# Attention block: x transposed mostly by transfers, late weights loaded later, one of 24 planned orders built

## The chip, the cores and the metric

The kernel runs on one core of a Trainium2 chip. The time is device microseconds of one execution; the median of three executions before the change is 361.78 us (361.48 to 361.86). The engines are called PE (TensorE, matrix products), ACT (ScalarE), DVE (VectorE), POOL (GpSimd) and SP (SyncE, which only issues transfers here).

## The reference

x is 2048 x 448, 16 heads of 28 columns each, all in bf16. There is no mask.

```
qkv = (x @ wqkv)                  # 448 -> 3 x 448, split into q, k, v per head
scores = q @ k.T * 28 ** -0.5     # 16 heads, 2048 x 2048 each
p = softmax(scores)               # over the keys
o = p @ v
out = o (heads side by side) @ wo
```

## The kernel before

**Tiling.** Heads are taken in four groups of four; a head has 32 rows (28 and 4 of padding) of the 128 partitions. Queries are cut into four chunks of 512 (c), keys into 16 tiles of 128, x into four blocks of 512 rows (b). A set is one group and one query chunk: 16 sets, each with 4 heads x 16 key tiles = 64 halves of 128 keys by 512 queries. There are 1024 halves.

**Start.** x is loaded row by row (L140) and transposed by PE with an identity (L621), 16 transposes of 128 x 112 per block, since the 448 columns are cut into four parts of 112. ACT copies the first half of a block from PSUM to SBUF (L629), DVE the second (L627); the result is XT. Then come the projections. `mm_proj` (L298) makes K and Q of a group with 16 matmuls per block of 512 (four parts of the columns, four heads); for group 0 it reads WG, an early load of the few weight columns needed, and later WRAW, the full weights (L136). `v_job` (L305) makes V. `k_first` makes K of group 0 for one block, with its square (L324), the norm over a head (L409) and its maximum (L414). `q_job` and `qn_first` make the first Q and its norm; the bound from both norms is subtracted from the scores through spare rows of Q, so that no maximum over the scores is taken. QP holds Q with these rows. It is cleared by DVE (L194), gets constant rows by 16 small transfers on SP (L198, from a tile offs), the rows of Q by four (L661) and the bound's rows, su, by two (L502). Until all this has landed, the first set's scores are made in two matmuls, from z and from su, in place of one from QP.

**Main phase.** A scores step (`emit_s`, L730) makes two halves for ACT, and often one for DVE. ACT takes the exponential of two halves at a time (L928, 128 x 1024). DVE makes an approximate exponential of one half by integer arithmetic (L943), with two shifted copies of four halves (L1014, or for one of them a clear and an accumulating transfer by POOL, L979 and L990) that are averaged in the next product. `do_pv` (L1073) multiplies with V. When a set is complete, its sum is divided: a gather and a scatter on SP, a reciprocal on DVE, four broadcasts on SP (rr) and a product on POOL (L1123). When a query chunk has all groups, `oproj_job` multiplies by WO and stores the rows. Row p*16 + 4*b + t of x, and of the output, belongs to partition p and column t of block b.

**Order.** The order of the instructions is written by a planner within the kernel: it keeps a clock for each engine (`free`), a table of times at which events happen (`evt`), durations as constants, and picks for the engine that is earliest the next operation by priority. Loads enter as fixed times. The planner fixes the order in each engine's queue; on the chip each engine runs its queue in order and waits on semaphores. `dve_ok` decides whether DVE takes another half; `pick_dve` sends a shifted copy ahead when it is older than AGE (2.5 us).

```
for n, t in (("x", 0), 4.9), (("G", 1), 6.9), (("G", 0), 6.9), (("x", 1), 6.2), (("x", 2), 8.0), (("x", 3), 9.3), \
        (("W", 2), 10.9), (("W", 0), 12.0), (("W", 1), 13.2):
    evt[n] = (t, "DMA")
```

**Queues at the start.** SP issues half of each x block, one WG, the three WRAW, L198, L661 and L502 in this order; ACT issues the other halves and the other WG, then loads its table. POOL clears V (L209, L210), clears WO (L216) and loads it with 16 transfers (L219).

Of the kernel before, what the change touches and what calls it, by code (L numbers as in the profile page):

```python
# [16 lines left out]
LAT = 0.2  # L17
# [20 lines left out]

@with_exitstack
def kernel(  # L40
# [16 lines left out]
    CK = D // CC  # L57
# [11 lines left out]
    NXB = NKT // XB  # L69
    SHIFT = (0, 43, 85)  # L70
# [20 lines left out]
    NSET = G * NQC  # L91
    GH = 2
# [6 lines left out]
    out_perm = out2.rearrange("(p t) d -> p t d", t=NKT)  # L99
# [7 lines left out]
    XT = [[big.tile([CK, CC // 2, QW], BF16, name=f"XT{b}_{k}") for k in range(2)] for b in range(NXB)]  # L107
# [15 lines left out]
    xs = [big.tile([P, XB, D], BF16, name=f"xs{b}") for b in range(NXB)]  # L123
    QP = [[[big.tile([P, QW], BF16, name=f"QP{c}_{k}_{z}") for z in range(2)] for k in range(2)] for c in range(NQC)]
    OTL = [big.tile([P, QW], BF16, name=f"OTL{c}") for c in range(NQC)]

    def otile(g, c):
        if g < G - 1:
            return xs[c][:].rearrange("p t d -> p (t d)")[:, g * QW:(g + 1) * QW]
        return OTL[c][:]  # L130

    wq3 = wqkv.rearrange("(cc p) n -> p cc n", p=CK)
    x3 = x2.rearrange("(p t) c -> p t c", t=NKT)

    def load_w(t, eng):
        eng.dma_start(out=WRAW[t][:, :, 0:D], in_=wq3[:, :, t * D:(t + 1) * D])  # L136

    def load_x(b, eng, k=0, n=1):
        w = XB // n
        eng.dma_start(out=xs[b][:, k * w:(k + 1) * w, :], in_=x3[:, b * XB + k * w:b * XB + (k + 1) * w, :])  # L140

    def load_w0(t, eng):
        eng.dma_start(out=WG[t], in_=wq3[:, :, t * D:t * D + HG * Dh + WPAD])
# [33 lines left out]
    offs = wk.tile([P, 2 * QW], BF16, name="pt", bufs=NPT)[0:2, 0:QW]  # L177
# [12 lines left out]
    nc.vector.memset(offs, OFFS)  # L190
    for c in range(NQC):
        for k in range(2):
            for z in range(2):
                nc.vector.memset(QP[c][k][z][:], 0.0)  # L194
    for z in range(2):
        for c in range(NQC):
            for k in range(2):
                nc.sync.dma_start(out=QP[c][k][z][HP * k + Dh + NQC - 1 - c:P:2 * HP, :], in_=offs)  # L198
# [4 lines left out]
    for t in range(3):  # L203
        nc.gpsimd.memset(WRAW[t][:, :, D:D + WPAD], 0.0)

# [9 lines left out]
    for gg in range(G):  # L215
        nc.gpsimd.memset(WO[:, gg, :], 0.0)  # L216
    for h in range(H):
        g, i = divmod(h, HG)
        nc.gpsimd.dma_start(out=WO[HP * i:HP * i + Dh, g, :], in_=wo[h * Dh:(h + 1) * Dh, :])  # L219
# [7 lines left out]
    def pair_tile(tg):  # L227
        return psum.tile([P, 2 * QW], F32, name=tg, tag=tg, bufs=1)

    def bank_tile(tg):  # L230
        return psum.tile([P, QW], F32, name=tg, tag=tg, bufs=1)


    free = {"PE": 0.0, "ACT": 0.0, "DVE": 0.0, "SP": 0.0, "POOL": 26.0}
    port = {"DVE": 0.0, "POOL": 0.0}
    evt = {}
    res = {"a0": 0.0, "a1": 0.0, "d0": 0.0, "d1": 0.0, "o": 0.0, "m": 0.0}
    ops = {"PE": [], "ACT": [], "DVE": [], "SP": [], "POOL": []}
    cnt = {"step": 0, "half": 0}
    held = {}  # L240
    cur = {"c_end": 0.0, "s": 0, "u": 0, "o": None, "oset": 0, "pv": 0, "half": 0, "o_open": False}
    parts = {}

    def add(eng, dur, emit, **k):
        op = Op(eng, dur, emit, **k)
        ops[eng].append(op)
        return op

    def ready(op):
        if cnt["step"] < op.gate or (op.acq == "m" and op.gives[0][0] == "O" and left() < OLAST):  # L250
            return None
        if op.acq == "m" and op.pri > 5 and ("KN0", NQC - 1) not in evt:
            return None
        r = 0.0
        for n in op.need:
            if n not in evt:
                return None
            t, e = evt[n]
            r = max(r, t + (0.03 if e == op.eng else LATS.get((e, op.eng), LAT)))
        if op.acq is not None:  # L260
            if res[op.acq] is None:
                return None
            r = max(r, res[op.acq])
        return r + op.lag

    def run(op, t):
        op.emit()
        if op.eng == "PE":
            note(t, op.cols)
        end = t + op.dur  # L270
        if op.eng == "PE" and main_on():
            cur["c_end"] = end
        if op.port:
            port[op.eng] = end
        for n in op.gives:
            evt[n] = (end + op.land, op.eng)
        if op.after is not None:
            op.after(end)
        if op.acq is not None:
            res[op.acq] = None  # L280
        if isinstance(op.rel, tuple):
            parts.setdefault(op.rel[0], []).append(end + LATS.get((op.eng, "PE"), LAT))
            if len(parts[op.rel[0]]) == op.rel[1]:
                res[op.rel[0]] = max(parts.pop(op.rel[0]))
        elif op.rel is not None:
            res[op.rel] = end + LATS.get((op.eng, "PE"), LAT)
        ops[op.eng].remove(op)
        return end


    KAt, QAt, sqt, kst, kmt = {}, {}, {}, {}, {}

    def mm_proj(ps, t, g, c, ccs):
        for cc in ccs:
            for i in range(HG):
                h = g * HG + i
                w = WG[t] if g == 0 else WRAW[t]
                nc.tensor.matmul(out=ps[HP * i:HP * (i + 1), :], lhsT=w[:, cc, h * Dh:h * Dh + HP],  # L298
                                 rhs=XT[c][cc // 2][:, cc % 2, :], start=(cc == 0), stop=(cc == CC - 1),
                                 tile_position=(0, HP * i))  # L300

    def quarters(out, lhsT, rhs, start, stop, **k):
        for i in range(P // HP):
            r = slice(HP * i, HP * (i + 1))
            nc.tensor.matmul(out=out[r, :], lhsT=lhsT[:, r], rhs=rhs, start=start, stop=stop, tile_position=(0, HP * i), **k)  # L305

    def after_shared(m):

        if "shared" in cur:
            tc.add_manual_dep(m.ins, cur["shared"].ins.name,  # L310
                              mybir.DependencyInfo(mybir.DependencyClass.Sync, mybir.DependencyReason.DATA),
                              reason="GpSimd's pass stays behind VectorE's")

    def new_sq(key):
        sqt[key] = wk.tile([P, QW], BF16, name="sq", tag="sq", bufs=4)
        return sqt[key]

    def square(key, src):
        t = new_sq(key)
        after_shared(nc.gpsimd.tensor_tensor(out=t[:], in0=src, in1=src, op=ALU.mult))  # L320

    def act_square(key, mask):
        t = new_sq(key)
        nc.scalar.activation(out=t[:], in_=held[key][:, 0:QW], func=ACT.Square, scale=mask[:, 0:1])  # L324

    def k_job(g, sc, bank, pri, gate=0, split=2):
        key = ("K", g, sc)
        n = CC // split

        def mm(part):  # L330
            if part == 0:
                held[key] = bank_tile(bank) if bank[0] != "a" else pair_tile(bank)
            mm_proj(held[key][:, 0:QW], 1, g, sc, range(part * n, (part + 1) * n))

        def evac():
            KAt[(g, sc)] = big.tile([P, QW], BF16, name=f"KA{sc}", tag=f"KA{sc}", bufs=2)
            src = held[key][:, 0:QW]
            nc.vector.tensor_scalar(out=KAt[(g, sc)][:], in0=src, scalar1=kmask[:, 0:1],  # L338
                                    scalar2=ones[:, 0:1], op0=ALU.mult, op1=ALU.add)

        for p in range(split):
            add("PE", n * D_WAVE, lambda p=p: mm(p), pri=pri, gate=gate, cols=448 * n,
                need=[("XT", sc, 0), ("XT", sc, 1), ("W", 1)] + ([key + (p - 1,)] if p else []), gives=[key + (p,)],
                acq=bank if p == 0 else None)
        add("DVE", 0.72, evac, need=[key + (split - 1,)], gives=[key], rel=bank, pri=pri)
        add("POOL", 1.08, lambda: square(key, KAt[(g, sc)][:]), need=[key], gives=[("ksq", g, sc)], pri=pri, port=True)

    def kn_job(g, bank, pri, gate=0):
        key = ("KN", g)

        def mm(sc):
            if sc == 0:
                held[key] = bank_tile(bank) if bank[0] != "a" else pair_tile(bank)
            quarters(held[key][:, 0:QW], maskK[:, sc, :], sqt.pop(("K", g, sc))[:], sc == 0, sc == NQC - 1)
# [1026 lines left out]
```

## Time and profile before

| | |
|---|---|
| median of 3 executions | 361.78 us |
| profiled execution | 361.72 us |
| its span, first to last instruction | 359.9 us |
| granted clock of PE | 0.998 of full speed |
| exponentials on ACT (L928) | 358, 329.7 us, with pairs of halves |
| halves on DVE (L943) | 308 (278 from d, 30 from m) |
| first exponential / last ends | 19.39 us / 351.3 us |
| POOL's set-up ends | 23.0 us |

The span is shorter than the time by what lies around the first and the last instruction. Busy time is the sum of an engine's instructions within the span; a group of the profile joins the instructions of one line, engine and operation, with their count, their mean duration and the idle time ahead of them. The chain of waits goes back from the last instruction to what released each step. SPq and ACTq are transfers being issued from the queues of SP and ACT; such an issue occupies the queue, and the transfer lands later.

### The profile page before, as it was taken

Reading aid. Unit: us, or ns where it says so; the run is one execution under the profiler, and the core shown is the slowest. Engines: PE = TensorE matmul, PEld = TensorE weight load, DVE = VectorE, ACT = ScalarE, POOL = GpSimd, SP = SyncE. Lnnn points to the kernel's source line nnn. Section 1 sums busy time; section 2 is a strip of 40 time slices with the busy share of each in tenths; the row PEclk is TensorE's granted clock in tenths of the full one; section 3 lists DMA queues with packets and bytes.
Section 4 is the critical chain, followed back from the end, with each engine's and each line's share of the span. In section 5 each row is a group of like instructions: output and inputs, shape, how many; then the busy total and the mean of one; then the engine's idle time right before and its main releaser. Section 6 shows DMA issues by size and latency. Waiting matters only on the chain.

```text
span 359.9 us, 11256 instructions
## 1 busy us (share of the span) xinstructions
PE 343.1 (95%) x4520; PEld 111.3 (31%) x4521; DVE 335.4 (93%) x617; ACT 341.1 (95%) x373; POOL 170.2 (47%) x213
## 2 busy tenths in 40 slices
PE   8999999999999999999999999999889999999995
PEld 4533233332234322332232222222222222222233
DVE  8689999999989999999899999999999999999863
ACT  3789999999999999999999999999999999999991
POOL 8951353655444483545635765465546362521010
PEclk9999999999999999999999999999999999999999
DMA  8620063555636765365577646377857685672111
GB/s 242 142 47 15 21 125 86 113 107 105 135 75 129 148 124 113 89 132 108 117 143 149 120 91 137 78 152 158 177 116 156 128 176 129 142 147 66 34 51 54
DMA packets 24017, 41.17 MB, mean 114 GB/s; under 512 B 8604, under 2 KB 15004, under 8 KB 23964
## 3 DMA queue, kind: packets, MB, share of 16 engines
q0 software_dynamic: 8432, 29.24, 42.0%
q1 hardware_dynamic: 14348, 10.07, 10.3%
q10 hardware_dynamic: 1184, 1.14, 1.0%
q8 instruction: 35, 0.57, 0.6%
q14 instruction: 18, 0.15, 0.1%
HBM read 7.58 MB, written 1.96 MB: 27 GB/s over the span
## 4 chain that ended last, share of the span: by engine, by line
PE 37%; ACT 30%; DVE 23%; issue 9%; DMA 1%; DVEq 0%; ACTq 0%
ACT pt L928 30%; PE a L730 12%; DVE I L943 10%; PE o L1073 10%; PE m L305 5%; DVE J L1014 5%; PE m L298 4%; DVE V L579 2%; DVE V L566 2%; DVE KA L338 1%; PE o L643 1%; PE d L730 1%; DVE QA L460 1%; DVE o_sb L1100 1%; PE d L621 1%
## 5 line engine op out<-in xcount | busy, mean ns | idle before, releaser
L928 ACT ACTIVATE pt<-a 128x1024 bf16<-128x1024 f32 x358 | 329.7, 1129 | 2.9 <-PE a L730 1.3
L943 DVE TENSOR_SCALAR I<-d 128x512 int16<-128x512 f32 x278 | 181.0, 680 | 10.1 <-PE d L730 8.8
L730 PE MATMUL a<-QP,KA 32*128 32x512 bf16 (+1 forms) x704 | 137.3, 381 | 8.9 <-ACT pt L928 8.0
L1073 PE MATMUL o<-pt,V 128*32 128x512 bf16 x716 | 105.2, 384 | 0.0
L730 PE MATMUL d<-QP,KA 32*128 32x512 bf16 (+1 forms) x273 | 95.7, 383 | 0.8 <-DVE I L943 0.2
L730 PEld LDWEIGHTS <-KA 32*128 32x128 bf16 (+1 forms) x1041 | 46.1, 91 | 143.5 <-issue 141.7
L990 POOL DMA_DIRECT2D J<-I x55 | 49.6, 902 | 73.0 <-DVE I L943 49.6
L1073 PE MATMUL o<-J,V 128*32 128x512 bf16 x616 | 82.7, 384 | 0.0
L979 POOL MEMSET J<- 128x1024 int32 x55 | 60.1, 1094 | 36.7 <-PE d L730 12.0
L1014 DVE TENSOR_SCALAR J<-I 128x2048 int16<-128x2048 int16 x99 | 73.9, 764 | 0.6
L1073 PE MATMUL o<-I,V 128*32 128x512 bf16 x308 | 64.3, 384 | 0.1
L1073 PEld LDWEIGHTS <-V 128*32 128x32 bf16 x1640 | 30.8, 94 | 48.2 <-issue 45.1
L1123 POOL TENSOR_TENSOR xs<-o_sb,rr 128x512 bf16<-128x512 f32 x12 | 16.9, 1404 | 27.3 <-DVE J L1014 26.9
L298 PE MATMUL m<-XT,WRAW 112*32 112x512 bf16 x384 | 29.6, 384 | 0.2 <-DVE QA L460 0.2
L320 POOL TENSOR_TENSOR sq<-QA 128x512 bf16<-128x512 bf16 x15 | 16.8, 1122 | 23.1 <-DVE QA L460 17.8
L305 PE MATMUL m<-WRAW,XT 112*32 112x112 bf16 (+1 forms) x768 | 20.7, 230 | 0.3 <-DVE KA L338 0.3
L943 DVE TENSOR_SCALAR I<-m 128x512 int16<-128x512 f32 x30 | 20.3, 678 | 0.0
L320 POOL TENSOR_TENSOR sq<-KA 128x512 bf16<-128x512 bf16 x12 | 14.2, 1185 | 9.4 <-DVE J L1014 8.5
L305 PEld LDWEIGHTS <-XT 112*32 112x32 bf16 x768 | 12.3, 96 | 11.5 <-issue 11.4
L305 PE MATMUL m<-WO,xs 128*32 128x448 bf16 x156 | 12.5, 358 | 0.0
L730 PE MATMUL m<-QP,KA 32*128 32x512 bf16 (+1 forms) x30 | 11.5, 384 | 0.0
L460 DVE CAST QA<-m 128x512 bf16<-128x512 f32 x15 | 10.2, 683 | 0.7 <-PE m L298 0.7
(116 smaller groups left out, 207.3 us busy)
## 6 DMA issues: line engine op xcount, KB each, us to landing
J<-I POOLq DMA_DIRECT2D x55, 512.0 KB, 4.9
rr<-scr SPq DMA_DIRECT2D x60, 64.0 KB
QP<-QA SPq DMA_DIRECT2D x60, 28.0 KB
out_dram<-osb SPq DMA_DIRECT2D x12, 112.0 KB
WRAW<-in_wqkv_dram SPq DMA_DIRECT2D x3, 392.0 KB
xs<-in_x_dram ACTq DMA_DIRECT2D x4, 224.0 KB
xs<-in_x_dram SPq DMA_DIRECT2D x4, 224.0 KB
QP<-su SPq DMA_DIRECT2D x32, 2.0 KB
```

What stands on the lines that cost most here:

```text
L298: nc.tensor.matmul(out=ps[HP * i:HP * (i + 1), :], lhsT=w[:, cc, h * Dh:h * Dh + HP], rhs=XT[c][cc // 2][:, cc % 2, :], start=(cc == 0), s ...
L305: nc.tensor.matmul(out=out[r, :], lhsT=lhsT[:, r], rhs=rhs, start=start, stop=stop, tile_position=(0, HP * i), **k)
L320: after_shared(nc.gpsimd.tensor_tensor(out=t[:], in0=src, in1=src, op=ALU.mult))
L460: nc.vector.tensor_copy(out=t[:], in_=held[key][:, 0:QW])
L730: nc.tensor.matmul(out=out_ap, lhsT=KAt[(g, j // XB)][r, (j % XB) * P:(j % XB + 1) * P], rhs=q[r, :], start=(n == 0), stop=(n == len(terms ...
L928: nc.scalar.activation(out=pt[:], in_=ps[:], func=ACT.Exp, scale=LN2 / 128.0)
L943: nc.vector.tensor_scalar(out=dst, in0=pd[:], scalar1=BIAS, scalar2=0.0, op0=ALU.add, op1=ALU.max)
L979: m = nc.gpsimd.memset(ch[1][:].bitcast(I32), fill)
L990: after_shared(nc.gpsimd.dma_start(out=ch[1][:, w], in_=ch["I"][:, w], accum_op=ALU.add))
L1014: cur["shared"] = nc.vector.tensor_scalar(out=r[:, w], in0=ch["I"][:, w], scalar1=float(SHIFT[k]), scalar2=None, op0=ALU.add)
L1073: nc.tensor.matmul(out=o[HP * i:HP * (i + 1), :], lhsT=VT[e["k"]][g, j // XB][:, j % XB, HP * i:HP * (i + 1)], rhs=e["ap"], start=(SETMM[k ...
L1123: m = nc.gpsimd.tensor_tensor(out=otile(g, c), in0=st["o_sb"][:], in1=st["rr"][:], op=ALU.mult)
```

## The change

- x: block 0 is loaded and transposed by PE as before, in parts of 128 columns (0, 128, 256 and 320 on; the last part overlaps the third by 64 columns). Blocks 1 to 3 come transposed by transfers on SP: one for columns 320 to 447 of all three blocks (XE), and one per block for columns 0 to 383. The weights' last part has zeros in its first 64 rows, so each projection still has four parts.
- Rows: block b is now rows 512*b to 512*b + 511; for blocks 1 to 3 row t*128 + p belongs to partition p. The output is stored in the same way.
- Weights: each load is two transfers; both WG go to ACT's queue. W0 and W1 are issued on SP after QP is complete for the first set.
- QP: half of it is cleared by POOL, and 14 of the 16 small transfers go to POOL's queue. offs has its own tile.
- WO: its clears wait for the last Q of group 0; its 16 loads go to SP in the planned part and the output projection waits for them.
- Planner: other due times, other PSUM banks for the first norms, QPRI 3.05; the whole plan is a function, run 24 times without emitting anything, with a random term in `dve_ok` (up to 0.4 us) and in the age (up to 1 us) except for number 0, and then once for the number whose latest engine clock is earliest.

The diff, without the lines that only move to the right:

```
-    CK = D // CC
+    CK = P
+    CT = D - CK
+    NPL = 1
+    NSEED = 24
-    out_perm = out2.rearrange("(p t) d -> p t d", t=NKT)
+    def out_at(c, tq, n=1):
+        o = out2[c * QW:(c + 1) * QW]
+        o = o.rearrange("(p t) d -> p t d", t=XB) if c < NPL else o.rearrange("(t p) d -> p t d", p=P)
+        return o[:, tq:tq + n, :] if n > 1 else o[:, tq, :]
...
+    def load_w(t, eng, n=D):
+        dst = WG[t] if n < D else WRAW[t][:, :, 0:D]
+        cols = slice(t * D, t * D + n)
+        eng.dma_start(out=dst[:, 0:CC - 1, :], in_=wqkv[0:(CC - 1) * CK, cols].rearrange("(cc p) n -> p cc n", p=CK))
+        eng.dma_start(out=dst[CC * CK - D:CK, CC - 1, :], in_=wqkv[(CC - 1) * CK:D, cols])
+    def load_x(b):
+        rows = slice(b * QW, (b + 1) * QW)
+        nc.sync.dma_start_transpose(out=XT[b][:], in_=x2[rows, 0:(CC - 1) * CK])
-    load_x(0, nc.sync, 0, 2)
-    load_x(0, nc.scalar, 1, 2)
-    for b in range(1, NXB):
-        load_x(b, nc.sync, 0, 2)
-        load_x(b, nc.scalar, 1, 2)
-        if b == 1:
-            load_w0(1, nc.sync)
-            load_w0(0, nc.scalar)
+    for b in range(NPL):
+        for eng, k in ((nc.sync, 0), (nc.scalar, 1)):
...
+    for t in range(2):
+        nc.vector.memset(WG[t][0:CC * CK - D, CC - 1, :], 0.0)
+    for t in (1, 0):
+        load_w(t, nc.scalar, HG * Dh + WPAD)
+    nc.sync.dma_start_transpose(out=XE[:], in_=x2[NPL * QW:S, CT:D])
+    for b in range(NPL, NXB):
+        load_x(b)
     load_w(2, nc.sync)
-    load_w(0, nc.sync)
-    load_w(1, nc.sync)
...
-            for z in range(2):
-                nc.vector.memset(QP[c][k][z][:], 0.0)
-    for z in range(2):
-        for c in range(NQC):
-            for k in range(2):
-                nc.sync.dma_start(out=QP[c][k][z][HP * k + Dh + NQC - 1 - c:P:2 * HP, :], in_=offs)
+            nc.vector.memset(QP[c][k][0][:], 0.0)
+    nc.gpsimd.memset(offs[:], OFFS)
+    offs_rows(0, 0, nc.sync)
...
+        nc.gpsimd.memset(WRAW[t][0:CC * CK - D, CC - 1, 0:D], 0.0)
...
+    for c in range(NQC):
+        for k in range(2):
+            nc.gpsimd.memset(QP[c][k][1][:], 0.0)
+    for z in range(2):
+        for c in range(NQC):
+            if c + z:
+                offs_rows(c, z, nc.gpsimd)
...
-    free = {"PE": 0.0, "ACT": 0.0, "DVE": 0.0, "SP": 0.0, "POOL": 26.0}
+    free = {"PE": 0.0, "ACT": 0.0, "DVE": 0.0, "SP": 0.0, "POOL": 25.6}
...
+    for n, t in [(("x", 0), 4.9), (("x", 1), 99.0)] + [(("XT", k, h), 8.9 + 1.8 * (k - NPL)) for k in range(NPL, NXB) for h in range(2)] + \
+            [(("G", 1), 6.7), (("G", 0), 6.7), (("W", 2), 14.2)]:
         evt[n] = (t, "DMA")
...
+    for gg in range(G):
+        add("POOL", 0.5, lambda gg=gg: clear_wo(gg), need=[("QA", 0, CL)], gives=[("WZ", gg)], pri=95, port=True)
+    for h in range(H):
+        add("SP", 0.55, lambda h=h: load_wo(h), need=[("WZ", h // HG)], gives=[("WO", h)], pri=9, land=2.5)
-    k_first(0, "a0", None, "DVE", "ACT", 1.5)
-    k_first(1, "a1", "o", "ACT", "ACT", 3.05, late=("ksq", 0, NQC - 1))
-    k_first(2, "d0", "a0", "ACT", "ACT", 3.1, late=("ksq", 0, NQC - 1))
-    k_first(3, "d1", "o", "DVE", "ACT", 3.2, late=("QA", 0, 0))
+    k_first(0, "a0", "o", "DVE", "ACT", 1.5)
+    k_first(1, "a1", "a0", "ACT", "ACT", 3.05, late=("ksq", 0, NQC - 1))
+    k_first(2, "d0", "o", "ACT", "ACT", 3.1, late=("ksq", 0, NQC - 1))
+    k_first(3, "d1", "a0", "DVE", "ACT", 3.2, late=("QA", 0, 0))
...
+    for t in range(2):
+        add("SP", 1.2, lambda t=t: load_w(t, nc.sync), need=["QP00"], gives=[("W", t)], land=6.0, pri=3)
...
-    return fin <= free["ACT"] + D_EXP * (len(exps) + max(0, left() // 2 - 2)) + 0.2
+    return fin <= free["ACT"] + D_EXP * (len(exps) + max(0, left() // 2 - 2)) + 0.2 + shake(0.4)
...
-    if can_add and t > adds[0][0]["at"] + AGE:
+    if can_add and t > adds[0][0]["at"] + AGE + shake(1.0):
...
+    d = Dry()
+    ends = {k: plan(d, d, d, d, d, d, k, True) for k in range(NSEED)}
+    seed = min(ends, key=lambda k: ends[k])
+    plan(nc, tc, psum, big, wk, dram, seed, False)
```

More of the change, by code (lines that the diff above doesn't have):

```diff
@@ L1 @@
+import random
 from contextlib import ExitStack
@@ L266, in run @@
[L266 to L288, printed above, removed]
@@ L291 @@
[L291 to L305, printed above, removed]
@@ L307, in after_shared @@
[L307 to L346, printed above, removed]
@@ new lines, in turn, with do_s @@
+        def turn(t):
+            return max(t, cur["c_end"] + D_TURN)
+        def do_s(t):
+            s = act_set()
+            if s >= NSET:
+                return None
+            q = qa_ready(s)
+            if q is None or q > t:
+                return None
+            got = d_more(s, t, True) if left() >= 16 or chain["cur"] is not None else []
+            used = {g[2][1] for g in got}
+            step = []
+            for x in range(2):
+                own = [i for i in (2 * x, 2 * x + 1) if i not in used and remain[s][i]]
+                step.append(take(s, max(own, key=lambda i: (len(remain[s][i]), (i + cur["u"]) % 2))))
+            bank = s_bank()
+            ps = pair_tile(bank)
+            emit_s([(ps[:, k * QW:(k + 1) * QW], step[k]) for k in range(2)] + [(g[1][:], g[2]) for g in got], t)
+            outst[s] += 2
+            res[bank] = None
+            t = turn(t)
+            end = t + D_S
+            exps.append((end + LATS[("PE", "ACT")], ps, bank, step))
+            cur["u"] += 1
+            cnt["half"] += 2
+            return max(end, put_d(got))
@@ new lines, in close, with used_up, j1_free, add_ok @@
+        def close(ch, m):
+            ch["m"] = m
+            ch["at"] = free["DVE"]
+            adds.append([ch, m, 2 if ch["far"] else 1])
+            if ch["far"]:
+                accumulate(ch, m)
+        def used_up(ch, k):
+            return ch["m"] is not None and ch["got"][k] == ch["m"]
+        def j1_free():
+            return len(chain["all"]) < NJ or used_up(chain["all"][-NJ], 1)
+        def add_ok(a):
+            if a[2] == 1:
+                return True
+            n = chain["all"].index(a[0])
+            return n < NCH2 or used_up(chain["all"][n - NCH2], 2)
@@ new lines, in far_chain, with emit, accumulate, landed @@
+        def far_chain(ch):
+            n = len(chain["all"])
+            fill = SHIFT[1] * 65537
+            def emit():
+                m = nc.gpsimd.memset(ch[1][:].bitcast(I32), fill)
+                after_shared(m)
+            ch["id"] = n
+            add("POOL", 1.05, emit, gives=[("fill", n)], pri=20, port=True)
+        def accumulate(ch, m):
+            w = slice(0, m * QW)
+            ch["acc"] = None
+            def emit():
+                after_shared(nc.gpsimd.dma_start(out=ch[1][:, w], in_=ch["I"][:, w], accum_op=ALU.add))
+            def landed(end):
+                at = ch["acc"] = end + ACC_LAND
+                for n in range(m):
+                    pending.append({"step": ch["steps"][n], "k": 1, "ap": ch[1][:, n * QW:(n + 1) * QW].bitcast(BF16),
+                                    "ready": at, "pt": None, "ch": ch})
+            evt[("I4", ch["id"])] = (free["DVE"], "DVE")
+            add("POOL", 0.88, emit, need=[("fill", ch["id"]), ("I4", ch["id"])], gives=[("acc", ch["id"])], pri=10, port=True)
+            ops["POOL"][-1].after = landed
@@ new lines, in flush, with do_add @@
+        def flush():
+            ch = chain["cur"]
+            if ch is not None and ch["done"] == ch["n"] and not any(remain[ch["s"]]):
+                chain["cur"] = None
+                close(ch, ch["n"])
+        def do_add(t):
+            ch, m, k = adds[0]
+            w = slice(0, m * QW)
+            if k == 2:
+                ch[k] = wk.tile([P, HG * QW], I16, name="J2", bufs=NCH2)
+            r = ch[k]
+            cur["shared"] = nc.vector.tensor_scalar(out=r[:, w], in0=ch["I"][:, w], scalar1=float(SHIFT[k]), scalar2=None, op0=ALU.add)
+            end = port["DVE"] = t + m * QW * 0.00026 + 0.068
+            for n in range(m):
+                pending.append({"step": ch["steps"][n], "k": k, "ap": r[:, n * QW:(n + 1) * QW].bitcast(BF16),
+                                "ready": end + LATS[("DVE", "PE")], "pt": None, "ch": ch})
+            adds[0][2] += 1
+            if adds[0][2] == NTERM:
+                adds.pop(0)
+            return end
@@ new lines, in plan, with filler @@
+        if dry:
+            return max(free.values())
+        s = NSET - 1
+        g, c = set_gc(s)
+        o = cur["o"]
+        HW = QW // 2
+        banks = held["early"]
+        more = sorted((op for op in ops["PE"] if op.gives[0][0] == "E"), key=lambda op: op.gives[0][1:])
+        def filler(n, to=XB):
+            for op in [op for op in more if op.gives[0][1] < to][:n]:
+                op.emit()
+                more.remove(op)
+        osb_last = [VT[1][0, hf].rearrange("p t e -> p (t e)").bitcast(F32) for hf in range(2)]
```

1801 lines of the change are left out of this document (893 added, 908 removed).

## The prediction

> **What bounds the kernel now.** I read the page's busy shares and slices first, then ScalarE (ACT) by stretches, then the chain of waits over the first 20 us, then SyncE's (SP's) timeline. From the page, the busy shares and two rows of the slices (a digit is the busy share of 9 us, in tenths):
>
> ```profile
> PE 343.1 (95%) x4520; PEld 111.3 (31%) x4521; DVE 335.4 (93%) x617; ACT 341.1 (95%) x373; POOL 170.2 (47%) x213
> ...
> DVE  8689999999989999999899999999999999999863
> ACT  3789999999999999999999999999999999999991
> ```
>
> Three engines run at 93 to 95%, and ACT's only poor slices are the first three and the last. ACT alone, from its first exponential (19.39 us) on; the second figure after the stretch is busy time:
>
> ```profile
> 19.39:24.95 5.56, 4.90 (x6) 1.00 0.27 63
> 24.95:351.30 326.35, 324.78 (x353) 1.00 0.55 113
> 351.30:359.90 8.60, 0.97 (x2) 0.91 0.16 56
> ```
>
> From 24.95 to 351.30 us ACT idles 1.57 us in all. It runs 358 exponentials at 329.7 / 358 = 0.921 us each, back to back. So the end is the first exponential, plus some 332 us, plus a tail of 8.6 us. What can move is the first exponential, the 0.66 us lost in the ramp, and how many exponentials ACT is given. The chain of waits before the first one (start, duration, what):
>
> ```profile
> 9.00 1.03 PE d L621 x16
> 10.03 0.98 PE a L298 x16
> 11.01 0.58 PE o L621 x8
> 11.59 0.21 PE a L409
> 11.81 0.45 PE m L621 x8
> 12.25 0.98 PE d L298 x16
> 13.23 0.32 PE o L409
> 13.55 0.98 PE m L298 x16
> 14.53 0.32 PE a L409
> 14.85 1.01 PE d L298 x16
> ```
>
> L298 is a projection (K of blocks 1, 2, 3 and Q of block 0), L621 are TensorE's transposes of x, L409 the key norms. TensorE works without a pause until 15.86 us. From there to the first exponential lie 3.53 us (square, norm, maximum, root, scaling, first scores), which the change leaves as they are.
>
> **The change, part by part.**
>
> *Transposes taken away.* Blocks 1 to 3 lose 48 of 64 transposes, three copies on ACT (1.00 us, L629) and three on VectorE (DVE, 0.68 us, L627). Block 1's transposes lie before K0, which waits for DVE's copy of block 0 (7.20 + 0.66 = 7.86 us) anyway: worth nothing. Those of blocks 2 and 3 are the three L621 pieces above: 1.03 + 0.58 + 0.45 = 2.06 us. The copies lie beside TensorE's chain and count no more. TensorE would then end K3 at 15.86 - 2.06 = 13.80 us, and ACT would start at 17.33.
>
> *Transfers put in their place.* SP issues four transposing transfers: XE (128 columns of 1536 rows) and three blocks of 512 rows by 384 columns, 0.39 MB each, 1.57 MB together, beside and behind block 0 and the first weights (0.67 MB). The trace has no transposing transfer; the nearest rows are two of the transfers by microsecond (last figure GB/s) and one of the page's issues (KB each, us to landing):
>
> ```profile
> 4.00:5.00 1.00, 1.00 (x3) 0.29 (x2) 0.99 (x4) 0.01 (x1) 0.89 (x4) 1.00 1.06 382
> 13.00:14.00 1.00, 1.00 (x21) 0.40 (x17) 0.54 (x2) 0.69 (x1) 1.00 (x4) 1.00 0.57 126
> ...
> J<-I POOLq DMA_DIRECT2D x55, 512.0 KB, 4.9
> ```
>
> In the four microseconds before 4.00 us 30, 122 and 384 GB/s moved 0.54 MB, so the 0.67 MB are in by 4.35. At 382 GB/s the last block would land at 4.35 + 1.57/0.382 = 8.5 us. At the rate of the accumulating transfer (512 KB in 4.9 us, 107 GB/s) it would be 19.0. The planner is told 8.9, 10.7 and 12.5 for the three blocks, 193 GB/s. I take that value: it lies between the rows, and the same table in the kernel before gives 13.2 us for the last weights, where the second row shows the stream running dry. K3 then runs from 12.7 to 13.75, the same 13.8 that TensorE's own work gives. So the first exponential is forecast at 17.3, **2.06 us earlier**; bounds 2.06 (TensorE's own work ends last, however fast the transfers are) and -4.3 (the slow end, worked out below). The wait also holds TensorE's queue, but behind K3 stand only filler matmuls and the V projection, which needs the later W2 anyway (planned at 14.2, first used at 16.99 before).
>
> *Block 0.* Transposes give 128 columns where they gave 112 and the projections read 128 partitions where they read 112. The moving sides stay 128 and 512 wide, and the transposes' and projections' counts per block stay 16. I take no change; an excess of a seventh on 1.49 us of transposes would cost 0.2.
>
> *Queues at the start.* ACT issues five transfers (0.45 us each, L143) in place of five, and none behind two long x loads, so its table load (1.28 us, from 4.99) can only come sooner; the first copy at 6.53 covers it. SP loses 14 of the 16 issues of L198, three x loads, a first weight and W0 and W1, and gains 4 transposing issues and a second one for W2. Its timeline before, and the first scores of the one-pass form:
>
> ```profile
> 7.63 11.51 SPq L198 DMA_DIRECT2D QP<-pt  x16
> 19.24 3.22 SPq L661 DMA_DIRECT2D QP<-z  x4
> 22.56 1.09 SPq L502 DMA_DIRECT2D QP<-su  x2
> ...
> 25.15 0.39 PE L730 MATMUL a<-QP,KA 32*128 32x512 bf16 x2
> ```
>
> Until QP is filled, every scores step takes a second pass (z, then su; 0.21 us). L661 could go at 16.30, when z is ready, but waits behind L198 until 19.24. In the new order z is ready near 13, L661 ends near 16.5, su comes at 16.6, L502 ends at 17.7, and the one-pass form starts 1.5 us later (before: 23.65 to 25.15), at 19.2: some 1.9 us after the first exponential, not 5.8. Three of six two-pass steps go. ACT lost 0.66 us there and DVE idled 1.18 of 5 us (20 to 25); bounds 0 and 0.66 + 0.92 (one exponential that DVE takes over). I take three fifths of the first, **0.4 us**.
>
> *POOL.* Its set-up ended at 23.01. It loses 1.77 us (WO cleared) and 8.54 (16 issues, L219), and gains 0.5 (offs), three clears of WRAW (1.5 by L216's 0.49), eight of QP (4.3 by 0.54) and 14 issues (7.7 by 0.549): end at 26.7. Its first work after that stood at 30.08, and 2.5 us earlier it is 27.6: 0.9 us of cover. Without it, the square for Q of block 1 slips by the excess; its set starts near 40 us. No cost.
>
> *Late loads.* W0 and W1 (four issues, 0.33 to 0.49 us) go behind L502, with 6 us to land: near 26, first use 44.7 less 2.5. The 16 loads of WO go to SP: 16 x 0.55 = 8.8 us spread over a queue that mostly waits, needed only by the output projections of the late sets. The four clears (0.49 us) now share POOL's time with DVE's passes: at most 2 us of DVE, which idles 10.5 us between 25 and 340 (315 less 304.5 busy in that stretch). Zero, with -0.9 as the bound.
>
> *Output rows.* The same 896-byte rows in another order; the last but one store (224 KB) has twice the packets. It is issued 0.96 us before the last one: no cost, at most 0.2.
>
> *The plan.* Of 24 plans (jitter of 0.4 us on DVE's admission, 1 us on an age) the shortest by the planner's clock is built. A wait is not added; the whole order after 20 us changes. Priced by exponentials: a pair of halves given to DVE saves ACT 0.92 and costs DVE 2 x (0.68 + 73.9/308) = 1.84 us. With 10.5 us of idle DVE time, up to 3.8 pairs could go (-3.5 us); as many could come back. I take zero.
>
> Sum, against the profiled execution's own 361.72 (span 359.9 and 1.8 around it; the median stands 0.06 above it): 361.72 - 2.06 - 0.4 + 0.06 = **359.3**.
>
> **The rivals.**
>
> *Slow transposes (slower).* At 107 GB/s the last block lands at 19.0, K3 ends at 20.2, the first exponential comes at 23.7: 4.3 us late, 366. It decides from the point where K3 starts 0.4 us later than the 14.85 of before, a landing at about 15.1, which is 146 GB/s. For it: the stream fell from 382 to some 250 GB/s on the weights' shorter rows. Against: 107 includes a fixed part of the landing, about 2.0 us (L219's 24.5 KB), so the stream itself is faster. At the far end, 48 tiles of 32 KB one after another at those 2.0 us would take 96 us and give about 447. The Trainium skill ("VectorE: DVE Perf Modes", the three transpose paths) gives 1309 ns for a 128x128 transpose by DMA and 390 ns by TensorE, and advises TensorE where PSUM is a possible target; by that figure in series, an estimate, the 48 tiles take 63 us and the time is about 414. The trace agrees on TensorE only in order (219 ns each) and can't show the other.
>
> *The plan gives it back (no change).* The new order hands ACT three exponentials more (+2.76): 361.78 - 2.46 + 2.76 = 362.1. For it: idle DVE is only 3% of 25 to 340 us, so little decides it. Against: earlier scores give DVE time, not ACT.
>
> *The plan adds (faster).* Two pairs fewer on ACT: 359.3 - 1.84 = 357.5. For it: 10.5 us of idle DVE. Against: 24 close orders differ by the planner's clock, which counts 0.904 us for an exponential that takes 0.921.
>
> **How the numbers follow.** About 0.2% (0.7 us) is what a measurement of this kernel can tell from no change, so faster is under 361.06, slower over 362.50. The forecast has 0.60 (358.3 to 360.4 with its own bounds), the adding plan 0.11, slow transposes 0.14 (the tiles in series 0.02 of it), the plan that gives back 0.15 (0.09 within the limits, 0.05 above, 0.01 below). Faster 0.72, same 0.09, slower 0.19. The range leaves out the far part of the slow transposes (0.12) and the last of the adding plan (0.03): 356.6 to 363.2.
>
> **What would show it.** Right: K3's 16 matmuls ending near 13.8, the first exponential near 17.3, the one-pass scores from about 19, ACT without gaps from 23 on, 358 exponentials give or take one. Wrong: K1 to K3 waiting for a transfer beyond 15 us (slow transposes); 361 exponentials, or gaps of over 2 us in ACT's middle (the plan); SP still issuing transposes when z is ready (no gain in the ramp); POOL's set-up past 28 us.

## The result, and the profile after

The changed kernel takes 539.79 us (538.54 to 539.93), the kernel before 361.69 in the same executions: 1.4917 times as long (95% interval 1.4891 to 1.4943). The forecast was 359.3, with a range from 356.6 to 363.2. It was wrong in size and in sign.

The page of the changed kernel, busy shares and four rows of the slices (13.5 us each):

```profile
PE 341.2 (63%) x4454; PEld 109.7 (20%) x4454; DVE 333.6 (62%) x607; ACT 339.1 (63%) x370; POOL 222.6 (41%) x319
...
PE   8600000000000029999999999999999988899997
...
DVE  5500000000000019999999999999999999999994
ACT  3400000000000019999999999999999999999994
...
PEclk9755555555555559999999999999999999999999
```

The engines do the same work as before: ACT is busy 339.1 us (341.1 before), with 358 exponentials again. But TensorE, DVE and ACT stand still from the third slice to the fourteenth, and TensorE's clock stands at half there. The page's groups name who waited and what took its place:

```profile
L782 PE MATMUL a<-QP,KA 32*128 32x512 bf16 (+1 forms) x708 | 139.1, 384 | 185.4 <-DMA QP<-su 174.1
...
L255 POOL MEMSET WO<- 128x448 bf16 x100 | 47.1, 474 | 116.4 <-DMA WO<-in_wo_dram 116.4
...
WO<-in_wo_dram SPq DMA_DIRECT2D x400, 24.5 KB
```

The scores waited 174.1 us for one transfer, su into QP. And WO, which has four column groups and 16 heads, is cleared 100 times and loaded by 400 transfers: 25 copies of 4 and 16. SP's timeline (start, length of the stretch, issues) shows how the two hang together, with the scores that were released:

```profile
10.33 1.22 SPq L225 DMA_DIRECT2D QP<-offs  x2
26.51 24.01 SPq L259 DMA_DIRECT2D WO<-in_wo_dram  x55
...
192.56 3.24 SPq L711 DMA_DIRECT2D QP<-z  x4
195.91 1.10 SPq L548 DMA_DIRECT2D QP<-su  x2
...
198.08 0.68 PE L782 MATMUL a<-QP,KA 32*128 32x512 bf16 x2 [174.10 <-DMA QP<-su]
```

SP's queue is served in order. After offs, at 11.55 us, the loads of WO come first; the first of them waits for a clear, and POOL starts the clears at 26.02, when its set-up is done. Then load and clear wait for each other: a clear may not start before the loads of the copy ahead have landed, and the next loads not before the clear. L711, whose data z was ready at 11.2, is issued at 192.56.

**Why 25 copies.** The diff has it. `clear_wo` and `load_wo` are defined outside `plan`, so their `nc` is the kernel's. Inside `plan` the name `nc` is a parameter, a `Dry` object in the 24 trial plans; the operations that use that one emit nothing. These two don't use it:

```
    def clear_wo(gg):
        nc.gpsimd.memset(WO[:, gg, :], 0.0)
...
    def plan(nc, tc, psum, big, wk, dram, seed, dry):
...
            add("POOL", 0.5, lambda gg=gg: clear_wo(gg), need=[("QA", 0, CL)], gives=[("WZ", gg)], pri=95, port=True)
```

Every trial plan that schedules the operation emits it for real, ahead of the plan that is built. The account of the change above says that the trial plans emit nothing, and the prediction takes it for granted. That is not so.

What the change was to do at the start did happen. From the timeline of the changed kernel, K3's matmuls, DVE's scaling and the first exponentials, and at the end DVE's scaling in the kernel before:

```profile
12.49 0.83 PE L344 MATMUL d<-XT,o_sb 128*32 128x512 bf16 x12
13.15 0.39 PE L344 MATMUL d<-XE,o_sb 128*32 128x512 bf16 x4
...
15.91 2.06 DVE L542 TENSOR_SCALAR su<-V,kroot 128x512 bf16<-128x512 f32 x1
...
18.67 1.94 ACT L980 ACTIVATE pt<-a 128x1024 bf16<-128x1024 f32 x2 [2.36 <-PE a L782]
...
18.20 0.49 DVE L496 TENSOR_SCALAR su<-V,kroot 128x512 bf16<-128x512 f32 x1
```

K3 ends at 13.54 (15.86 before). But su takes 2.06 us, where the same operation took 0.49 before (L496), and the first exponential comes at 18.67. So there are two questions: do the copies explain the whole stall, and what holds su?

### The profile page after: what moved, and what is told of

Same layout as the page of the kernel before. It is cut to its first block, busy times and chain, and to the rows that moved or that the text cites. A ratio compares the mean times of both kernels' runs of the same rounds, so it can differ in the third digit from the quotient of the medians.

```text
span 538.0 us, 11904 instructions
## 1 busy us (share of the span) xinstructions
PE 341.2 (63%) x4454; PEld 109.7 (20%) x4454; DVE 333.6 (62%) x607; ACT 339.1 (63%) x370; POOL 222.6 (41%) x319
## 4 chain that ended last, share of the span: by engine, by line
PE 25%; ACT 23%; DMA 16%; SPq 11%; POOL 9%; issue 8%; DVE 7%; POOLq 1%; DVEq 0%; ACTq 0%
ACT pt L980 23%; DMA WO<-in_wo_dram 14%; SPq L259 10%; PE a L782 9%; PE o L1125 8%; POOL WO L255 4%; PE m L351 4%; DVE I L995 3%; PE m L344 3%; DVE J L1066 2%; POOL V L240 1%; POOL QP L225 1%; DMA rr<-scr 1%; DMA scr<-rec 1%; POOL QP L248 1%
## 5 line engine op out<-in xcount | busy, mean ns | idle before, releaser
L782 PE MATMUL a<-QP,KA 32*128 32x512 bf16 (+1 forms) x708 | 139.1, 384 | 185.4 <-DMA QP<-su 174.1
L1125 PE MATMUL o<-pt,V 128*32 128x512 bf16 x716 | 109.0, 387 | 0.0
L782 PE MATMUL d<-QP,KA 32*128 32x512 bf16 (+1 forms) x273 | 99.2, 387 | 0.1
L255 POOL MEMSET WO<- 128x448 bf16 x100 | 47.1, 474 | 116.4 <-DMA WO<-in_wo_dram 116.4
L1125 PE MATMUL o<-J,V 128*32 128x512 bf16 x616 | 87.2, 385 | 0.4 <-DVE J L1066 0.4
L1031 POOL MEMSET J<- 128x1024 int32 x55 | 58.4, 1061 | 48.7 <-PE d L782 13.5
L1042 POOL DMA_DIRECT2D J<-I x55 | 52.6, 957 | 57.9 <-DVE I L995 49.8
L1125 PE MATMUL o<-I,V 128*32 128x512 bf16 x308 | 69.2, 387 | 0.9 <-DVE o_sb L1152 0.8
L1175 POOL TENSOR_TENSOR xs<-o_sb,rr 128x512 bf16<-128x512 f32 x12 | 17.1, 1427 | 29.4 <-DVE J L1066 20.1
L344 PE MATMUL m<-XT,WRAW 128*32 128x512 bf16 x216 | 18.3, 386 | 0.1
L351 PE MATMUL m<-WRAW,XT 128*32 128x112 bf16 (+1 forms) x432 | 14.5, 243 | 0.2
L351 PE MATMUL m<-WO,xs 128*32 128x448 bf16 x156 | 12.5, 359 | 0.0
L351 PE MATMUL m<-sq,maskK 128*32 128x512 bf16 x108 | 10.8, 389 | 1.4 <-POOL sq L366 1.4
```

What stands on the lines that cost most here:

```text
L782: nc.tensor.matmul(out=out_ap, lhsT=KAt[(g, j // XB)][r, (j % XB) * P:(j % XB + 1) * P], rhs=q[r, :], start=(n == 0), stop=(n == len(terms ...
L1031: m = nc.gpsimd.memset(ch[1][:].bitcast(I32), fill)
L1042: after_shared(nc.gpsimd.dma_start(out=ch[1][:, w], in_=ch["I"][:, w], accum_op=ALU.add))
L1125: nc.tensor.matmul(out=o[HP * i:HP * (i + 1), :], lhsT=VT[e["k"]][g, j // XB][:, j % XB, HP * i:HP * (i + 1)], rhs=e["ap"], start=(SETMM[k ...
```

## The experiments

Line numbers differ by a few between these kernels; the operations are named.

### One part of the copies: leak8, leak1

```
-    def clear_wo(gg):
+    def clear_wo(nc, gg):
...
+    NC = nc
     def plan(nc, tc, psum, big, wk, dram, seed, dry):
...
-        lambda gg=gg: clear_wo(gg)
+        lambda gg=gg: clear_wo(NC if dry and seed < 8 else nc, gg)     # load_wo alike; leak1: seed < 1
```

> The same order of the main work as the changed kernel (plan 14); the clears and loads of WO are emitted by 8 of the 24 trial plans in place of all 24. Theory A (each trial plan emits its clears and loads for real, and these stand ahead of the rows of the first Q on SP): the 166 us from 26.5 to 192.5 us are 24 copies of 6.9 us, so 16 copies fewer give 539.8 - 16 x 6.9 = 429 us, with 144 WO transfers. Rival B (one copy of the 16 loads on SP, or their place in the queue, is enough to cause the wait): still about 540. Rival C (the transposing transfers or PE's lowered clock make the stall): still over 500.

> Plan 14 again, with the clears and loads of WO emitted by one trial plan. 24 and 8 copies gave 539.8 and 428.5 us, 6.96 us a copy; on that line one copy gives 379.8 and none 372.9, while none gave 363.7. Theory A1 (a fixed part of some 9 us comes with the first copy, since SP stands from z on until POOL's set-up ends at 26 us, and TensorE's clock has then to come back): 378 to 382. Theory A2 (copies cost 7 us each and nothing else): 371.

Each was executed once: leak8 took 428.54 us (429 expected), leak1 381.65 (378 to 382). From 24 to 8 copies a copy costs (539.79 - 428.54) / 16 = 6.95 us, from 8 to 1 (428.54 - 381.65) / 7 = 6.70. leak1's SP shows one copy and what it holds up:

```profile
10.51 1.23 SPq L225 DMA_DIRECT2D QP<-offs  x2
26.46 6.79 SPq L259 DMA_DIRECT2D WO<-in_wo_dram  x16
33.35 3.24 SPq L713 DMA_DIRECT2D QP<-z  x4
```

A copy is 6.79 us of SP's queue; the wait from 11.7 to 26.46 comes with the first copy. leak1 less one copy is 374.9, 11 us over the kernel without copies (363.67, next): that is the fixed part. It fits the traces: the transfer of su is issued at 36.69 us in leak1 and at 17.99 in the kernel without copies, 18.7 later, and the time is 18.0 longer. Rivals B (540 with any copy) and C (over 500) fall by these times; the transposing transfers are in all of these kernels. B was right in one thing: the first copy alone brings the fixed part.

### No copies: fix, and plan 0: fix_seed0

```
-            add("POOL", 0.5, lambda gg=gg: clear_wo(gg), ...
+            add("POOL", 0.5, lambda gg=gg: clear_wo(nc, gg), ...
...
-            add("SP", 0.55, lambda h=h: load_wo(h), ...
+            add("SP", 0.55, lambda h=h: load_wo(nc, h), ...
```

fix_seed0 has NSEED = 1 besides.

> The changed kernel with the clears and loads of WO emitted only by the plan that is built (16 loads, 4 clears); everything else as in the changed kernel. Theory A: the stall goes whole. The first exponential stays at 18.7 us, since it lies before the stall, 0.7 us earlier than before, and the ramp gains up to 0.4: 360.6 us. If DVE's su still waits for POOL's clears of QP and TensorE's clock still falls to half near 20 us, some microseconds are lost in the ramp: 361 to 364. Rival B or C: 500 or more. The forecast's own sum was 359.3.

> As fix, but only plan 0 (no random terms) is made and built. By the planner's clock plan 0 ends 1.7 us after the chosen plan 14 (347.3 and 345.6). If that clock orders plans as the chip does: 1.7 us over fix. If reordering is worth nothing on the chip, as the prediction took it: within 0.7 us of fix.

fix took 363.67 us, 1.0082 times before (1.0049 to 1.0116); fix_seed0 363.89, 1.0071 (1.0043 to 1.0099). The two are 0.2 us apart, as expected if the order of plans is worth nothing on the chip; the planner's clock had them 1.7 apart (more on this below). The stall is gone: the copies cost 539.79 - 363.67 = 176.1 us, 24 x 6.9 and a fixed part. What is left is still slower than before, as the worse branch of the expectation had it. The windows of fix (busy time of PE, PEld, DVE, ACT and POOL, then the granted clock):

```profile
15.00:16.00 1.00, 0.77 (x14) 0.20 (x3) 0.93 (x3) 0.68 (x2) 1.00 (x3) 1.00 0.12 31
16.00:17.00 1.00, 0.00 (x0) 0.00 (x0) 1.00 (x1) 0.00 (x0) 1.00 (x3) 1.00 0.11 29
17.00:18.00 1.00, 0.00 (x0) 0.00 (x0) 1.00 (x2) 0.00 (x0) 1.00 (x3) 0.96 0.03 8
18.00:19.00 1.00, 0.99 (x8) 0.44 (x8) 1.00 (x3) 0.00 (x0) 1.00 (x3) 0.50 0.02 2
```

TensorE stands still for 2.2 us while DVE is "busy" with su, and comes back at half its clock, which lasts until about 28 us. This is the one execution of fix with a trace. Of nine executions of fix, three ran at a mean clock of 0.983 to 0.986 and took 366.5 to 367.6 us; the other six, at 0.993 to 1.000, took 363.0 to 364.1. The long fall of the clock thus goes with 3 to 4 us, but fix is slower than before without it too.

### What holds su: fix_dve, fix_clear16, fix_clear8x2

fix_dve undoes one part of the change, POOL's clears of half of QP; the other two make each of these clears twice.

```
fix_dve
-            nc.vector.memset(QP[c][k][0][:], 0.0)
+            for z in range(2):
+                nc.vector.memset(QP[c][k][z][:], 0.0)
...
-            nc.gpsimd.memset(QP[c][k][1][:], 0.0)
fix_clear16
+            for _ in range(2):
                 nc.gpsimd.memset(QP[c][k][1][:], 0.0)
fix_clear8x2
+    for _ in range(2):
         for c in range(NQC):
             for k in range(2):
                 nc.gpsimd.memset(QP[c][k][1][:], 0.0)
```

> As fix, but the eight clears of QP that the change gave to POOL are on DVE again, ahead of the others. Theory D (DVE's su took 2.06 us in place of 0.49 because it ran beside POOL's eight clears, which ended at 17.70, and TensorE sat idle for it): su takes 0.5 us, the first exponential comes at 17.1 us, TensorE's clock stays whole: 1.6 us or more faster than fix, near 359.0. Rival (su's length has another cause, such as the scores beside it): first exponential at 18.7, same time as fix.

> As fix, but each of POOL's eight clears of QP is made twice: POOL's row of clears ends 3.9 us later, near 21.6 us in place of 17.6. Theory D (DVE's su can't go while POOL clears follow one another, and starts work at their end): su, issued near 15.4, ends near 21.8 and takes some 6.4 us, the first exponential comes at 22.5 to 23.0, TensorE's clock falls in every execution, and the time is 4 us or more over fix: 367 to 371. Rival (each clear slows su by a share, with the length of su set by something else): su stays at 2.1 to 2.6 us and the time within 1 us of fix.

> The same 16 clears of QP on POOL as in fix_clear16, in another order: the eight tiles in turn and then again, so that no clear follows one of the same tile. In fix the eight clears start every 0.48 us and last 0.53 to 0.60, so each overlaps the next; in fix_clear16, where each tile is cleared twice running, they start every 0.56 us and su took only 0.71. Theory E (DVE's pass gets in where two clears don't overlap, and waits through every pair that does): su waits until the row of 16 ends near 21.6 us, some 6 us long, the first exponential at 22.5 or later, and 4 us or more over fix. Rival F (the number of clears or their order has nothing to do with su; it is short or long by chance of the moment): su between 0.5 and 2.6 us, first exponential before 19.5.

fix_dve took 360.81 us, 0.9981 (0.9971 to 0.9990), 2.9 less than fix. The end of its K3, its su, its first exponentials and its first scores in one pass (from QP):

```profile
13.12 0.39 PE L342 MATMUL d<-XE,o_sb 128*32 128x512 bf16 x4
...
15.88 0.49 DVE L540 TENSOR_SCALAR su<-V,kroot 128x512 bf16<-128x512 f32 x1
...
17.06 1.94 ACT L978 ACTIVATE pt<-a 128x1024 bf16<-128x1024 f32 x2 [0.79 <-PE a L780]
19.19 48.38 ACT L978 ACTIVATE pt<-a 128x1024 bf16<-128x1024 f32 x52 [0.19 <-PE d L780]
...
20.70 0.39 PE L780 MATMUL a<-QP,KA 32*128 32x512 bf16 x2
```

That is theory D's result at the start (17.1), though not its time (359.0; below). But fix_clear16 went against theory D: with twice as many clears it took 362.69, less than fix. Its su was shorter, too, than the rival there had it (2.1 to 2.6 us). Here are POOL's row of clears and su, for fix, fix_clear16 and fix_clear8x2 (start, length); for fix_clear16 also POOL's busy time in a stretch of 0.05 us:

```profile
13.81 3.87 POOL L248 MEMSET QP<- 128x512 bf16 x8
...
15.38 2.58 DVE L542 TENSOR_SCALAR su<-V,kroot 128x512 bf16<-128x512 f32 x1
```

```profile
13.83 9.02 POOL L249 MEMSET QP<- 128x512 bf16 x16
...
16.11 0.71 DVE L543 TENSOR_SCALAR su<-V,kroot 128x512 bf16<-128x512 f32 x1
...
16.54:16.59 0.05, 0.00 (x0) 1.00 0.00 0
```

```profile
13.81 7.60 POOL L249 MEMSET QP<- 128x512 bf16 x16
...
15.81 5.88 DVE L543 TENSOR_SCALAR su<-V,kroot 128x512 bf16<-128x512 f32 x1
```

In fix a clear lasts 0.53 to 0.60 us and the next starts after 3.87 / 8 = 0.48: they overlap. In fix_clear16 each tile is cleared twice running, and between two clears of the same tile POOL is idle for 0.06 us, as in the stretch shown; su gets through in 0.71. The same 16 clears in the other order overlap again (every 0.47), and su lasts until the row ends: 5.88 us, 370.91 us in all (two executions), 1.0245 (1.0189 to 1.0301), as theory E said. The ends agree to 0.01 us. In all five traced kernels with the row of eight (changed, leak8, leak1, fix, fix_seed0) su begins anywhere from 15.38 to 15.91 and ends 0.28 us after the row, in fix_clear8x2 again 0.28 after the row, and in fix_clear16 0.28 after the gap at 16.54. So it isn't the clears that hold DVE but a row of them without a gap. The Trainium skill ("SBUF — State Buffer", section "SBUF: two separate sides") says that certain passes of DVE and any operation of GpSimd share one pair of ports, by an exclusive lock for the whole instruction. The traces agree that su is blocked and not merely slowed: it ends with the row whenever it began. They add that the wait is not for one instruction (0.55 us) but for the whole row (su took 5.88), where the instructions overlap; which lock passes from one to the next, no run here shows.

### What the transposing transfers bring: dve_pe4

fix_dve with all blocks transposed by TensorE:

```
-    NPL = 1
+    NPL = 4
...
-    nc.sync.dma_start_transpose(out=XE[:], in_=x2[NPL * QW:S, CT:D])
-    for b in range(NPL, NXB):
-        load_x(b)
```

> As fix_dve, but all four blocks of x are loaded by rows and transposed by TensorE, with the due times of the kernel before; the early weights go on both queues after block 1, and offs lies in a tile of the pool pt, for space. The forecast's step: the transposes of blocks 2 and 3 on TensorE cost 2.06 us of the first exponential (17.1 becomes 19.1), so 2.1 us over fix_dve, 362.9. Rival (the gain at the start is given back in the middle whatever the start, since DVE or TensorE has as little room as ACT): first exponential near 19.1 but the time within 0.7 us of fix_dve's 360.8.

363.03 us, 1.0036 (1.0022 to 1.0049): 2.2 over fix_dve (2.0 by the two ratios to before), where the forecast's step was 2.06. Two lines of its trace, the start of K0 and the first exponentials:

```profile
8.53 1.05 PE L339 MATMUL a<-XA,o_sb 128*32 128x512 bf16 x16 [0.93 <-ACT XA L672]
...
19.90 1.94 ACT L975 ACTIVATE pt<-a 128x1024 bf16<-128x1024 f32 x2 [0.79 <-PE a L777]
```

The first exponential came at 19.90, in fix_dve at 17.06, 2.84 earlier. Not all of that is the transposes: K0, which comes ahead of the transposes of blocks 2 and 3, began at 8.53 here, after a wait for ACT's copy of block 0, and at 7.58 in fix_dve. Without these 0.95 us, 1.89 are left at the first exponential. So the agreement of 2.2 with 2.06 is in part luck; that the transposes are worth about 2 us at the start is what the two kernels show.

The transfers were no limit. Four microseconds of the changed kernel in which they run (last figure GB/s), and the packets that were moved from 9.5 to 11.36 us:

```profile
5.00:6.00 1.00, 1.00 (x7) 0.59 (x6) 0.00 (x0) 0.00 (x0) 0.88 (x4) 1.00 1.34 224
8.00:9.00 1.00, 1.00 (x27) 0.58 (x20) 0.00 (x0) 0.29 (x1) 0.94 (x4) 1.00 1.17 263
9.00:10.00 1.00, 1.00 (x26) 0.51 (x20) 0.57 (x1) 0.82 (x2) 0.94 (x3) 1.00 0.66 93
10.00:11.00 1.00, 0.94 (x14) 0.23 (x8) 0.88 (x2) 0.82 (x2) 0.94 (x3) 1.00 1.14 253
...
DMA packets 1458, 0.41 MB, mean 218 GB/s; under 512 B 1394, under 2 KB 1458, under 8 KB 1458
```

Between 4 and 9 us the stream, with the first weights' transfers in it, runs at 224 to 274 GB/s. The transposing transfers move in packets of 256 bytes, 6144 of them for their 1.57 MB; W2, issued behind them on SP, moves in packets of 896. From 9.5 to 11.36 us 1394 of 1458 packets are under 512. The last of the four transfers runs from 8.95 to 11.35 us: it begins slowly, in the row at 9 us, and has the next microsecond to itself. K3's matmuls start at 12.49, 1.1 us after its last packet; TensorE is busy until then with its own work.

### The choice of a plan: dve_plan0, dve_plan15, dve_plan18, dve_plan20

```
-    seed = min(ends, key=lambda k: ends[k])
+    seed = 18          # 0, 15, 20
```

> As fix_dve, but plan 0 is built (by the planner's clock 347.32, the chosen plan 14 has 345.60). If the planner's clock holds on the chip: 1.7 us over fix_dve, 362.5. If orders differ on the chip by something the clock doesn't see: anywhere within 1.5 us of 360.8, and no nearer to 362.5 than to 359.1.

> As fix_dve, but plan 15 is built, the last of the 24 by the planner's clock (348.67, 3.1 us after plan 14). If the clock holds on the chip: 363.9. If not: within 1.5 us of 360.8.

> As fix_dve, with plan 18 (345.79 by the planner's clock, 0.2 us after plan 14). The clock did not order plans 14 and 0 on the chip. What counts by the traces so far: the first exponential near 17.1, 0.92 us for each of ACT's exponentials, and its gaps. If the planner's clock holds: 361.0. If not: 360 to 361.5.

> As fix_dve, with plan 20 (346.25 by the planner's clock, 0.65 us after plan 14). If the planner's clock holds: 361.5. If not: 360 to 361.5.

| plan (all as fix_dve) | planner's end | median us | ratio to before, 95% interval | first exponential |
|---|---|---|---|---|
| 14 (chosen) | 345.60 | 360.81 | 0.9981 (0.9971 to 0.9990) | 17.06 |
| 18 | 345.79 | 358.08 | 0.9904 (0.9887 to 0.9920) | 16.52 |
| 20 | 346.25 | 359.30 | 0.9940 (0.9924 to 0.9957) | 16.93 |
| 0 (no random terms) | 347.32 | 360.69 | 0.9970 (0.9958 to 0.9981) | 17.12 |
| 15 (last of 24) | 348.67 | 361.45 | 0.9999 (0.9979 to 1.0020) | 17.17 |

Four of the five stand in the planner's order, but its first choice is not among them: plan 14 takes 2.7 us more than plan 18, 0.2 us behind it by the clock, and as much as plan 0, 1.7 behind. Plans differ by 3.4 us on the chip, which is more than the transposes bring. Plans 0 and 15 came out as expected if the planner's clock doesn't hold; plans 18 and 20 lie below both values that were expected of them (360 to 361.5). One of plan 15's ten executions took 529.84 us at a whole clock; no trace of it was kept, and the ratio leaves it out. The first exponential is no property of the plan: in the traces of plans 14, 18, 20 and 0 it comes 10.55 us after ACT's first copy of block 0, and that copy began between 5.97 (plan 18) and 6.57 (plan 0). The plan-18 kernel is faster than both kernels, by 3.5 us on before. ACT alone, in fix_dve and then in dve_plan18, from the end of the ramp to the last exponential:

```profile
24.95:349.86 324.91, 322.61 (x351) 1.00 0.56 115
```

```profile
24.95:347.17 322.22, 321.42 (x350) 1.00 0.55 115
```

Plan 14 leaves ACT idle for 2.30 us there, plan 18 for 0.80 (before: 1.57). Both give ACT 358 exponentials; plan 0 gives it 360. From the first exponential to the end of the last, plan 14 needs 332.80 us and plan 18 330.65; the other 0.54 of plan 18's lead in these traces is its earlier start. Why plan 14's order runs into more gaps than its own clock saw was not traced.

## Why the prediction was wrong

**The step that failed is "Late loads"**: "The 16 loads of WO go to SP: 16 x 0.55 = 8.8 us spread over a queue that mostly waits". They are 400 loads and 100 clears, and 384 of the loads stand in SP's queue ahead of L711, which waited for them until 192.56 us. The step counted what a plan adds and not what the 24 trial plans emit. None of the rivals had this, so the range didn't either. It cost 176 of the 178 us; the rest of the sum can be read from fix_dve and its kin.

**"POOL ... No cost" failed too.** The sum of POOL's durations held (26.7 forecast; in the changed kernel the last piece ends at 26.1), and so did the cover of its successors (in fix POOL's next work waits 6.35 us for DVE). What was left out is whom POOL's eight clears would meet: su on DVE, the last step before the first exponential. With that part undone, 2.9 us.

**Transposes: right.** The forecast had K3 ending at 13.8 and the first exponential at 17.3; in fix_dve K3 ended at 13.51 and the first exponential came at 17.06. The extra 0.3 us comes from K0, which began at 7.58, not at 7.95 as before. Slow transposes, at 0.14, didn't come: the last packet was through at 11.35 us, where a landing at 15.1 was the point of decision and 12.5 the value taken. The far end, 48 tiles in series, is refuted: from first packet to last the 48 tiles took 7.7 us. The Trainium skill ("VectorE: DVE Perf Modes", the three transpose paths) gives 1309 ns for a tile; at 7.7 us for 48 the trace shows that this is not the time from one tile to the next. The Trainium skill ("DMA: Bandwidth & Descriptors", section "Latency and other measured facts") states 261 GB/s for transposing transfers of one layout. The trace comes near it where a transposing transfer runs alone, 253 GB/s from 10 to 11 us; from first packet to last it is 205.

**Ramp: right, but only in fix_dve.** ACT idled 0.22 us between its first exponential and 24.95, not 0.66: 0.44 gained, 0.4 forecast. ACT alone in that stretch of fix_dve:

```profile
17.06:24.95 7.89, 7.67 (x9) 1.00 0.43 110
```

The way there was not the forecast one: scores in one pass were to start at 19.2 and started at 20.70, 3.6 us after the first exponential and not 1.9. The close value is luck in part.

**The plan, taken at zero: mis-sized.** In profiled executions fix_dve gained 361.72 - 360.54 = 1.18 us of the 2.46 forecast. Its first exponential came 2.33 earlier. From there to the end of the last one it needs 332.80 us (before 331.87), 0.93 more although the ramp gained 0.44; the tail is 8.94 (8.64). So the order of the middle gave back 0.93 + 0.44 = 1.37 and the tail 0.30. With plan 18 the middle gave nothing back, and the time, 358.1, is 1.2 under the forecast; but plan 18 is the best of five that were measured, and not the one that the kernel builds. The rival "the plan gives it back" had the mechanism right in part: by gaps in plan 14, by two more exponentials in plan 0.

## What to carry to other kernels

When a schedule is tried with stand-in objects before it is emitted, look for every emitting function that is defined outside and holds the real engine: count an instruction in the profile (x400 where 16 are meant) before asking what an engine waits for. Work that is moved to a half-idle engine has a price at the moments when it shares something with the engine on the path, and there a row of overlapping operations is worse than the same work with gaps. Plans that differ by tenths on a planner's clock can differ by microseconds on the chip: measure several, don't build the first.

## What was not expected of the hardware

- DVE's pass of 0.49 us took 5.88 beside 16 overlapping clears on POOL and 0.71 beside the same 16 with gaps of 0.06 us.
- TensorE's clock fell to half after a pause of 2.2 us in the traced execution of fix; three of its nine executions have such a low mean clock and took 3 to 4 us longer, three have a mean clock of 1.000. In the changed kernel a pause of 1.7 us (16.31 to 18.02) was enough: the clock was at half from 19.9 on. The Trainium skill ("TensorE: Matmul & The Clock Gate", Part 1) gives a window of about 3.4 us that runs freely, and a fall after an idle one. The pauses here are shorter than that, so if such a window is at work, it need not be idle throughout; that the clock falls in some executions and not in others would fit a window that the kernel doesn't set.
- In the profiled execution of plan 15 the clock stood at 0.85 from near the start to the end, and the time was 364.63 us, 3.2 over the median of that kernel: 15% of TensorE's clock cost under 1% of the time, though TensorE is busy for 96% of the span.
